# mLSTM cell and gated MLP on one core: seven-product up-projection from the middle of the second chunk, GpSimd's sums re-laid

## The chip, the cores and the metric

The kernel runs on one core of a Trainium2 chip. The metric is the device time of one execution in microseconds (us). The kernel before has a median of 506.22 us in three runs (503.96 to 506.45).

## The reference, cut to what matters

Two blocks follow each other. The first is an mLSTM cell over 768 time steps for 4 x 8 heads of dimension 40; the second is an MLP over the 3072 rows that come out.

```python
for t in range(S):                       # S = 768, per batch and head
    m_new = max(f + m, i)                # running maximum of the gates
    C = exp(f + m - m_new) * C + exp(i - m_new) * outer(v, k)
    n = exp(f + m - m_new) * n + exp(i - m_new) * k
    y[t] = sigmoid(o) * (C @ q) / max(|n . q|, 1)
x = y as (4 * 768, 320)
h = x @ w_in                             # 320 x 2048
out = (h * cos(h)) @ w_out               # 2048 x 320
```

All of it is float32.

## The kernel before, in words

**Chunks and cells.** Time is cut into NC = 6 chunks of 128 steps. A *cell* n = 4c + b is batch b of chunk c, its 8 heads together. A cell is computed in chunkwise form: scores q.k (`scores`, L560, TensorE), times a decay matrix E (`decay_exponents` on GpSimd, L462; `decay` on ScalarE, L476, eight exponentials; `weigh` on VectorE, L566), then `values` (TensorE, L586 to L595: E against v, and the carried state against qG, which `scale_q` makes on GpSimd, L542), `seam` (L701, the increment of the state), `normalize_turned` (VectorE, L613 to L638), `fade` (GpSimd, L684) and `state` (VectorE, L726). `turn_blocks` (VectorE, two transposes, L538) lays out q and k of the next cell.

**Up.** The 512 rows of a chunk (4 batches of 128) go through w_in in 8 *steps* f2 = 0 to 7; a step makes two tiles of 128 features by 512 rows in two PSUM banks. Step "2.6" below is chunk 2 (counted from 0), f2 = 6. In chunks 0 and 1 (class `Up`) a step is four products of 512 columns (two halves of the 256 main input rows, two tiles; L749) and two products over the 64 rows left (`w_in_l`, L743). Each float32 product stands as two matmul records in the trace. In chunks 2 to 5 (class `UpFast`) a step does the 2 x 2 block product with seven products of 256 columns (L817), and the 64-row products (L833). They need sums of blocks of w_in: S1, S2 and S4 in a tile `room`, and S3 written over the block A21 of w_in itself (`up_weight_sums`, L785 to L792, GpSimd), and sums of blocks of x: T1, T2, T4 in `x_room`, and one block of xT overwritten (`x_sums`, L801 to L804, GpSimd). After the first four products ScalarE copies both banks into a tile s (L825, L826), GpSimd makes three sums in s (L834 to L836), and `join` on VectorE (L842, L844) adds them back. TensorE goes on meanwhile with two products of the down-projection (`fill_in`, FILL = 2) and then the last three products of the step; the first of these three writes into the bank that L825 has copied.

**Gate.** h * cos(h) is `near` (ScalarE, L757), `rest` (VectorE, L760), `sin` (ScalarE, L765) and `gate` (L769 on VectorE; in `UpFast` the second tile's gate is on GpSimd, L852).

**Down.** Chunk 0 uses plain products (L863). Chunks 1 to 5 use a block scheme with seven products of 160 columns over sums of g (`sums`, four operations of VectorE, L902 to L905, or of GpSimd) and of w_out (`weight_sums`, GpSimd, L891 to L894, four parts for two pairs each). The products of pair k (L1014) come out of a generator, twelve for a pair, two records each; `down_slot` says how many a step takes. In chunk 1 step f2 takes the 12 products of pair f2 - 1.

**The order of the work** is written out by hand: every engine runs its instructions strictly in the order in which the program lists them. `both_parts` lists the work of one cell and two steps for chunk 1, `both_parts_fast` for chunks 2 to 5. In chunk 1 the cells 8 to 11 are computed, in chunk 2 the cells 12 to 15. The first pair of steps in `both_parts_fast` has a case of its own, `first`, since the scores of its cell are not there yet.

Of the kernel before, what the change touches and what calls it, by code (L numbers as in the profile page):

```python
# [16 lines left out]
OP = mybir.AluOpType  # L17
# [12 lines left out]
def kernel(  # L30
# [355 lines left out]
    def sigmoid_in_place(c):  # L386
        nc.scalar.activation(out=raw_o[c], in_=raw_o[c], func=AF.Sigmoid)
# [384 lines left out]
    wi = w_in_sb.rearrange("p i (f e n) -> p i f e n", e=2, n=128)  # L772
    A11, A12, A21, A22 = (wi[:, i, :, e] for e in range(2) for i in range(NK))
    HB = B // 2 * C
    fast = 2
    Sw, Tx = {}, {}
    x_room = const.tile([128, 3 * B // 2, C], FP, name="x_room")

    def up_weight_sums(part):

        tt = nc.gpsimd.tensor_tensor
        S1, S2, S4 = (room[:, i] for i in range(3))
        Sw[0] = S1, S2, S4, A21
        if part == 0:
            tt(out=S1, in0=A21, in1=A22, op=OP.add)  # L785
            tt(out=S2, in0=S1, in1=A11, op=OP.subtract)
        elif part == 1:
            tt(out=S4, in0=A12, in1=S2, op=OP.subtract)
        r = ((), range(0, 4), range(4, NF // 2))[part]
        if r:  # L790
            r = slice(r[0], r[-1] + 1)
            tt(out=A21[:, r], in0=A11[:, r], in1=A21[:, r], op=OP.subtract)  # L792

    def x_block(c, i, t):
        h = NK * B // 2
        return xT[c][:, i + h * t:h * (t + 1):NK]

    def x_sums(c):
        T1, T2, T4 = Tx[c] = x_room.rearrange("p (k b) t -> k p b t", k=3)
        tt = nc.gpsimd.tensor_tensor  # L800
        tt(out=T1, in0=x_block(c, 0, 1), in1=x_block(c, 0, 0), op=OP.subtract)  # L801
        tt(out=T2, in0=x_block(c, 1, 1), in1=T1, op=OP.subtract)
        tt(out=T4, in0=x_block(c, 1, 0), in1=T2, op=OP.subtract)
        tt(out=x_block(c, 0, 1), in0=x_block(c, 1, 1), in1=x_block(c, 0, 1), op=OP.subtract)  # L804

    class UpFast(Up):

# [72 lines left out]
    def out_to(c, b, o):  # L880
        nc.sync.dma_start(out=out[b * S + c * C:b * S + (c + 1) * C], in_=o)

    def weight_sums(part):

        if part == 0:
            for i in range(3):
                T[i] = pc.tile([128, NF // 2, HALF], FP, name=f"T{i}", tag="bits")
        r = ts(part, NF // 8)
        B11, B12, B21, B22 = (wv[:, r, e, h] for e in range(2) for h in range(2))
        T2, T3, T4 = (t[:, r] for t in T)  # L890
        nc.gpsimd.tensor_tensor(out=T3, in0=B22, in1=B12, op=OP.subtract)  # L891
        nc.gpsimd.tensor_tensor(out=B12, in0=B12, in1=B11, op=OP.subtract)
        nc.gpsimd.tensor_tensor(out=T2, in0=B22, in1=B12, op=OP.subtract)
        nc.gpsimd.tensor_tensor(out=T4, in0=B21, in1=T2, op=OP.subtract)  # L894

    def sums(c, k, engine=nc.vector):

# [113 lines left out]
    def run(made, n):  # L1011
        for _ in range(n):
            a, lhs, rhs, start, stop = next(made)
            nc.tensor.matmul(a, lhs, rhs, start=start, stop=stop)  # L1014
# [39 lines left out]

    def filled(c, f2):

        return c >= fast

    def products_of(c):
        if c not in made_of:  # L1060
# [7 lines left out]
    def down_slot(c, f2):  # L1068

        if c == 0:  # L1070
            if f2 > 0:
                down(0, f2 - 1)
            return
        if f2 == 0:
            if c == 1:
                down(0, LAST)
            else:
                run(made_of[c - 1], 12 - 2 * FILL)
            return
        if f2 == 1 and c > 1:  # L1080
            run(late_products(c - 1), NF)
            return
        each = 14 if c == NC - 1 else 12
        quota = [0] * 8
        for m in range(2, 8):
            quota[m] = each * 7 * (m - 1) // 6 - each * 7 * (m - 2) // 6
        if c == NC - 1:
            quota = [0, 0, 14, 14, 14, 14, 14, 21]
        run(products_of(c), each if c == 1 else quota[f2] - FILL * filled(c, f2))

    pw, pmu = (ps_u.tile([128, HP, C], FP, name=name, tag="up") for name in ("pw", "pmu"))

# [354 lines left out]
    def both_parts(c, b):  # L1447

        n = (c + 1) * B + b
        for i in range(2):  # L1450
            f2 = 2 * b + i
            up = Up(c, f2)
            if i == 0:
                scores(n)
            elif n % 2 == 1 and n + 3 < N:
                load_two(n + 3)
            for e in range(2):
                up.near(e)
            for e in range(2):
                up.rest(e)  # L1460
            if i == 0:
                weigh(n)
                decay_exponents(n + 1)
                for e in range(2):
                    up.sin(e)
                    up.gate(e)
                sums(c, f2)
                if b == B - 1:
                    sigmoid_in_place(c + 2)
                decay(n + 1)  # L1470
            else:
                seam_out(n)
                state(n)
                for e in range(2):
                    up.sin(e)
                    up.gate(e)
                sums(c, f2)
                weigh_k(n + 1)
                odd_values(n + 1)
            down_slot(c, f2)  # L1480
            if i == 0:
                values(n)
                seam(n)
                normalize_turned(n)
                fade(n)
                if b < 3:
                    weight_sums(b + 1)
                load_blocks(n + 2)
                load_E(n + 3)
                if b == B - 2:  # L1490
                    load_o(c + 2)
                sin_next()
            else:
                turn_blocks(n + 1)
                if n + 1 < (fast + 1) * B:
                    scale_q(n + 1)
                if b > 0:
                    up_weight_sums(b - 1)
                if b == B - 1:
                    x_sums(c + 1)  # L1500

    def both_parts_fast(c, b):

        n = (c + 1) * B + b
        cell, follows = n < N, n + 1 < N
        first = (c, b) == (fast, 0)
        ahead = {0: 3, B - 1: 2}.get(b, H - 2)
        pool = nc.gpsimd if cell else nc.vector
        for i in range(2):
            f2 = 2 * b + i  # L1510
            up = UpFast(c, f2, lambda: fill_in(c, f2))
            if f2 == 0:
                if cell:
                    place_gates(c + 1)
                if cell and not first:
                    weigh_k(n)
                sin_next()
            if f2 == 2 * B - 2 and c + 2 < NC:
# [2 lines left out]
            if cell and i == 0:  # L1521
                if first:
                    scores(n)
                    scale_q(n)
                else:
                    values(n)
                    seam(n)
                    if f2 > 0 and follows:
                        turn_blocks(n + 1)
                if follows:  # L1530
                    decay_exponents(n + 1)
            if cell and i == 1:
                if follows:
                    decay(n + 1, range(ahead, H))
                    sin_next()
                    if f2 > 1:
                        scores(n + 1)
                if n % 2 == 1 and n + 3 < N:
                    load_two(n + 3)
                if b == B - 1:  # L1540
                    x_sums(c + 1)
                    if follows:
                        scale_q(n + 1)
                elif follows:
                    weigh_k(n + 1)
                    odd_values(n + 1)
                    scale_q(n + 1)
                if b == 0:
                    if first:
                        fade(n)  # L1550
                    sums(c, 0, pool)
            up.join()
            if first and i == 0:
# [11 lines left out]
            for e in range(2):  # L1565
                up.sin(e)
                up.gate(e)
            if f2 == 0 and follows:
                turn_blocks(n + 1)
            if f2 == 1 and cell:  # L1570
                state(n)
            if f2 == 0 and not cell:
                sums(c, 0, pool)
            if f2 == 2:
                sums(c, 1, pool)
            down_slot(c, f2)
            if f2 == 1 and follows:
                scores(n + 1)
            if f2 == 0:
                for p in range(2):  # L1580
# [3 lines left out]
            if cell and i == 0:  # L1584
                if follows:
                    decay(n + 1, range(ahead))
                if first:
                    values(n)
                    seam(n)
                normalize_turned(n)  # L1590
                if n + 2 < N:
                    load_blocks(n + 2)
                if n + 3 < N:
                    load_E(n + 3)
                if b == B - 2 and c + 2 < NC:
                    load_o(c + 2)
            if i == 0:
                if f2 > 0:
                    if cell:
                        state(n)  # L1600
                    sums(c, f2)
            if i == 1:
# [12 lines left out]
    with tc.manual_schedule():  # L1615
        first_cells()
        first_period()
        for b in range(1, B):
            first_parts(b)
        for c in range(1, NC):  # L1620
            for b in range(B):
                (both_parts_fast if c >= fast else both_parts)(c, b)
        run(made_of[NC - 1], 21)
        combine_last()

# [29 lines left out]
```

## Time and profile before

The profiled execution took 503.72 us, with a span of 501.9 us between its first and its last instruction. The table gives, for each stretch of it, the busy time of each engine in us:

| Stretch | us | TensorE | VectorE | ScalarE | GpSimd |
|---|---|---|---|---|---|
| start, cells of chunk 0 | 31.9 | 30.32 | 26.02 | 24.53 | 16.45 |
| chunk 0 | 83.3 | 82.44 | 76.93 | 74.34 | 49.34 |
| chunk 1 | 76.8 | 76.80 | 64.78 | 47.64 | 48.10 |
| chunk 2 | 78.9 | 78.90 | 70.16 | 54.29 | 54.21 |
| chunk 3 | 78.0 | 77.99 | 69.44 | 55.15 | 56.86 |
| chunk 4 | 75.8 | 75.48 | 61.91 | 46.10 | 45.76 |
| chunk 5 and end | 77.2 | 73.19 | 51.36 | 30.44 | 29.32 |

How to read the profile: a busy TensorE says only that it has matmuls in flight, so the length of a step is read from the start of its first matmul to the start of the next step's. "Idle before" is the time that an engine stood still ahead of an instruction, and what ended it. A line of the timeline gives the start in us from the span's start, the length, the engine, the line of the program, the operation, and output and inputs.

### The profile page before, as it was taken

To read this page: it belongs to the slowest core of one execution; us is meant where nothing else is said; L and a number is where in the kernel's file an instruction comes from. 1 tells how busy PE (TensorE), PEld (TensorE's weight loads), DVE (VectorE), ACT (ScalarE), POOL (GpSimd) and SP (SyncE) were. 2 spreads that over 40 slices of the span, in tenths; PEclk is the share of its full clock that TensorE was granted. 3 is DMA by queue.
4 is the path that set the end of the run, shared out by engine and by line. 5 is a ranking of instruction groups with operands and counts; after the bars stand their busy time and mean duration, and the time that the engine had idled before them with its cause. 6 is when DMAs were issued, how large, how long until landed. Compare 5 with 4: busy or idle time off the path is not lost.

```text
span 501.9 us, 11143 instructions
## 1 busy us (share of the span) xinstructions
PE 495.1 (99%) x4038; PEld 375.4 (75%) x4038; DVE 420.6 (84%) x842; ACT 332.5 (66%) x646; POOL 300.0 (60%) x394
## 2 busy tenths in 40 slices
PE   9999999999999999999999999999999999999997
PEld 6856656565667668887887888788788888787876
DVE  7899998999878878899889889889979866777565
ACT  6799997878564575765877846777847743443541
POOL 8254557666555576787558877657567446434340
PEclk9999999999999999999999999999999999999999
DMA  9989899997366346129446118628113000010001
GB/s 139 182 223 239 213 224 279 233 217 136 114 178 111 101 120 127 50 86 202 132 125 106 48 54 195 168 83 150 43 35 85 1 7 5 2 54 0 2 0 54
DMA packets 100663, 56.74 MB, mean 113 GB/s; under 512 B 63456, under 2 KB 93360, under 8 KB 100608
## 3 DMA queue, kind: packets, MB, share of 16 engines
q1 hardware_dynamic: 97408, 54.43, 46.8%
q10 hardware_dynamic: 2896, 1.23, 1.0%
q8 instruction: 32, 0.52, 0.5%
q0 software_dynamic: 304, 0.36, 0.3%
q14 instruction: 23, 0.19, 0.1%
HBM read 50.66 MB, written 4.10 MB: 109 GB/s over the span
## 4 chain that ended last, share of the span: by engine, by line
PE 85%; ACT 4%; DVE 3%; DMA 2%; SPq 2%; POOL 2%; issue 1%; DVEq 0%; ACTq 0%; POOLq 0%
PE acc L1014 24%; PE pup L817 17%; PE pup L749 9%; PE po L863 6%; PE pup L833 6%; PE late L1014 5%; PE ps L560 4%; PE pup L743 3%; PE vt L595 2%; PE vt L586 2%; PE pu L701 2%; PE ph L576 1%; DMA E<-M_d 1%; DMA vs<-in_v_dram 1%; DVE n L760 1%
## 5 line engine op out<-in xcount | busy, mean ns | idle before, releaser
L757 ACT ACTIVATE n<-pup 128x512 int32<-128x512 f32 x64 | 37.0, 593 | 84.2 <-DVE pup L842 58.4
L765 ACT ACTIVATE n<-n 128x512 f32<-128x512 f32 x96 | 57.7, 626 | 16.5 <-DVE n L760 12.5
L852 POOL TENSOR_TENSOR g<-g,n 128x512 f32<-128x512 f32 x31 | 39.6, 1278 | 47.5 <-ACT n L765 47.4
L749 PE MATMUL pup<-xT,w_in_sb 128*128 128x512 f32 x128 | 58.7, 601 | 0.3 <-ACT xT L712 0.2
L1014 PE MATMUL acc<-w_out_sb,g 128*128 128x160 f32 x320 | 58.7, 303 | 0.0
L760 DVE SCALAR_TENSOR_TENSOR n<-pup,n 128x512 f32<-128x512 f32 x64 | 43.1, 689 | 18.5 <-ACT n L757 15.9
L834 POOL TENSOR_TENSOR blocks<-blocks 128x256 f32<-128x256 f32 x32 | 25.1, 785 | 54.5 <-ACT blocks L826 54.5
L1014 PE MATMUL acc<-T,g 128*128 128x160 f32 x304 | 56.4, 301 | 0.0
L817 PE MATMUL pup<-xT,w_in_sb 128*128 128x256 f32 x192 | 53.5, 385 | 0.2
L476 ACT ACTIVATE E<-E,tab 128x128 f32<-128x128 f32 x160 | 50.1, 389 | 4.3 <-POOL E L462 4.1
L1014 PEld LDWEIGHTS acc<-w_out_sb,g 128*128 128x128 f32 x320 | 49.0, 190 | 4.7 <-issue 2.7
L769 DVE TENSOR_TENSOR g<-pup,n 128x512 f32<-128x512 f32 x64 | 42.7, 687 | 5.7 <-ACT n L765 4.8
L1014 PEld LDWEIGHTS acc<-T,g 128*128 128x128 f32 x304 | 46.5, 190 | 1.1 <-issue 0.4
L749 PEld LDWEIGHTS pup<-xT,w_in_sb 128*128 128x128 f32 x128 | 23.1, 189 | 30.7 <-issue 30.0
L825 ACT COPY blocks<-pup 128x512 f32<-128x512 f32 x32 | 18.6, 582 | 34.2 <-PE pup L817 33.8
L817 PEld LDWEIGHTS pup<-xT,w_in_sb 128*128 128x128 f32 x192 | 33.8, 189 | 9.6 <-ACT blocks L826 4.4
L817 PE MATMUL pup<-x_room,room 128*128 128x256 f32 x128 | 38.5, 382 | 0.0
L542 POOL TENSOR_TENSOR qG<-t,G 128x512 f32<-128x512 f32 x20 | 26.4, 1321 | 16.7 <-DVE t L538 16.7
L1014 PE MATMUL acc<-T,blocks 128*128 128x160 f32 x160 | 36.2, 308 | 0.2 <-POOL blocks L904 0.2
L863 PE MATMUL po<-w_out_sb,g 128*128 128x320 f32 x128 | 36.2, 436 | 0.1
L833 PE MATMUL pup<-xL,w_in_l 64*128 64x512 f32 x128 | 36.1, 641 | 0.0
L566 DVE TENSOR_TENSOR E<-ps,E 128x512 f32<-128x512 f32 x46 | 29.5, 682 | 5.8 <-PE ps L560 5.6
(227 smaller groups left out, 1210.7 us busy)
## 6 DMA issues: line engine op xcount, KB each, us to landing
E<-M_d SPq DMA_DIRECT2D x20, 512.0 KB, 6.0
qr<-in_q_dram SPq DMA_DIRECT2D x72, 80.0 KB, 2.6
kr<-in_k_dram SPq DMA_DIRECT2D x72, 80.0 KB, 2.2
bits<-in_moe_w_out_dram SPq DMA_DIRECT2D x8, 640.0 KB, 6.2
G<-G_d SPq DMA_DIRECT2D x18, 256.0 KB, 5.7
blocks<-in_moe_w_in_dram SPq DMA_DIRECT2D x32, 128.0 KB, 4.6
out_dram<-o_sb SPq DMA_DIRECT2D x23, 160.0 KB, 1.8
o<-in_o_gate_dram SPq DMA_DIRECT2D x40, 80.0 KB, 4.4
```

The costliest lines, as they stand in the source:

```text
L476: nc.scalar.activation(out=Es[n][:, h], in_=Es[n][:, h], func=AF.Exp, scale=-1.0, bias=tab[:, c, 0, g:g + 1])
L566: nc.vector.tensor_tensor(out=w, in0=pss[n][j], in1=w, op=OP.mult)
L749: nc.tensor.matmul(pu.rearrange("p (b t) -> p b t", b=B), w_in_sb[:, i, ts(2 * f2 + e, 128)], xT[c][:, i:NK * B:NK], start=(i == 0 and not ...
L757: nc.scalar.activation(out=self.n[e], in_=self.pu[e], func=AF.Copy, bias=0.25)
L760: nc.vector.scalar_tensor_tensor(out=self.n[e].bitcast(FP), in0=self.pu[e], scalar=0.25, in1=self.n[e], op0=OP.add, op1=OP.subtract)
L765: nc.scalar.activation(out=r, in_=r, func=AF.Sin, scale=TWO_PI_DOWN)
L769: nc.vector.tensor_tensor(out=g, in0=self.pu[e], in1=self.n[e].bitcast(FP), op=OP.mult)
L817: nc.tensor.matmul(bank[:, part].rearrange("p (b t) -> p b t", b=B // 2), w[:, f2], x, start=start, stop=stop, skip_group_check=True)
L833: nc.tensor.matmul(pu, w_in_l[r, f2], xL[c][r].rearrange("p b t -> p (b t)"), start=False, stop=True, skip_group_check=True)
L852: tt(out=self.g, in0=self.g, in1=self.n[e].bitcast(FP), op=OP.mult)
L863: nc.tensor.matmul(po[c][b], gs[c, f][:, ts(b, C)], w_out_sb[:, f], start=(f == 0), stop=(f == NF - 1))
L1014: nc.tensor.matmul(a, lhs, rhs, start=start, stop=stop)
```

## The change

Chunk 1 goes over to seven products with its fifth step: `FAST = 1, B // 2`, so `both_parts_fast` runs from chunk 1, b = 2 (steps 1.4 to 1.7), and the case `first` moves there from chunk 2, b = 0. In `first`, `scale_q` is already done by `both_parts`, `turn_blocks` and `state` of the cell stand in steps 1.4 and 1.5, `fade` after `values`, and the next cell's scores after the slot of step 1.5, the odd one. The sums for w_in are made in halves over the feature pairs (4 and 4) and moved forward: S1 and S2 in step 1.0, S4, T1, T2, T4 and the upper half of S3 in step 1.2, the x block in step 1.3. The lower half of S3 overwrites what the plain steps 1.0 to 1.3 read, and is made in step 1.7, behind the gates. `weight_sums` of parts 1 and 2 move to steps 1.1 and 1.3, ahead of `scale_q`; part 3 is split over steps 1.5 and 1.6. Step 1.3 takes ten products in its slot in place of twelve, steps 1.4 to 1.7 take two as fill and ten in the slot, and step 2.0 takes two and ten in place of two and eight.

```diff
-    fast = 2
+    FAST = 1, B // 2
...
         Sw[0] = S1, S2, S4, A21
+        halves = slice(0, 4), slice(4, NF // 2)
         if part == 0:
-            tt(out=S1, in0=A21, in1=A22, op=OP.add)
-            tt(out=S2, in0=S1, in1=A11, op=OP.subtract)
+            for r in halves:
+                tt(out=S1[:, r], in0=A21[:, r], in1=A22[:, r], op=OP.add)
+            for r in halves:
+                tt(out=S2[:, r], in0=S1[:, r], in1=A11[:, r], op=OP.subtract)
         elif part == 1:
-            tt(out=S4, in0=A12, in1=S2, op=OP.subtract)
-        r = ((), range(0, 4), range(4, NF // 2))[part]
-        if r:
-            r = slice(r[0], r[-1] + 1)
+            for r in halves:
+                tt(out=S4[:, r], in0=A12[:, r], in1=S2[:, r], op=OP.subtract)
+        else:
+            r = halves[3 - part]
             tt(out=A21[:, r], in0=A11[:, r], in1=A21[:, r], op=OP.subtract)
...
     def filled(c, f2):
-        return c >= fast
+        return (c, f2 // 2) >= FAST
...
-                run(made_of[c - 1], 12 - 2 * FILL)
+                run(made_of[c - 1], 12 - FILL if c == 2 else 12 - 2 * FILL)
...
-        run(products_of(c), each if c == 1 else quota[f2] - FILL * filled(c, f2))
+        run(products_of(c), (each - FILL * (f2 > 2)) if c == 1 else quota[f2] - FILL)
...
# both_parts (chunk 1, now b = 0 and 1 only)
             if i == 0:
                 weigh(n)
                 decay_exponents(n + 1)
+                if b == 1:
+                    up_weight_sums(1)
+                    x_sums(c, [0])
...
                 sums(c, f2)
-                if b == B - 1:
-                    sigmoid_in_place(c + 2)
                 decay(n + 1)
...
                 fade(n)
-                if b < 3:
-                    weight_sums(b + 1)
+                up_weight_sums(2 * b)
                 load_blocks(n + 2)
                 load_E(n + 3)
-                if b == B - 2:
-                    load_o(c + 2)
                 sin_next()
             else:
                 turn_blocks(n + 1)
-                if n + 1 < (fast + 1) * B:
-                    scale_q(n + 1)
-                if b > 0:
-                    up_weight_sums(b - 1)
-                if b == B - 1:
-                    x_sums(c + 1)
+                if b == 1:
+                    x_sums(c, [1])
+                weight_sums(b + 1)
+                scale_q(n + 1)
...
# both_parts_fast
-        first = (c, b) == (fast, 0)
+        first = (c, b) == FAST
...
-                if cell and not first:
+                if cell:
                     weigh_k(n)
...
                 if first:
                     scores(n)
-                    scale_q(n)
...
-                    if f2 > 1:
+                    if f2 > 1 and not first:
                         scores(n + 1)
...
-                    if first:
-                        fade(n)
                     sums(c, 0, pool)
...
             for e in range(2):
                 up.sin(e)
                 up.gate(e)
-            if f2 == 0 and follows:
+            if c == 1:
+                if f2 in (5, 6):
+                    weight_sums(3, range(2 * f2 - 10, 2 * f2 - 8))
+                elif f2 == 7:
+                    up_weight_sums(3)
+            if (f2 == 0 or first and i == 0) and follows:
                 turn_blocks(n + 1)
-            if f2 == 1 and cell:
+            if (f2 == 1 or first and i == 1) and cell:
                 state(n)
...
-            if f2 == 2:
+            if f2 == 2 and c > 1:
                 sums(c, 1, pool)
             down_slot(c, f2)
-            if f2 == 1 and follows:
+            if (f2 == 1 or first and i == 1) and follows:
                 scores(n + 1)
...
                 if first:
                     values(n)
                     seam(n)
+                    fade(n)
...
-                    if cell:
+                    if cell and not first:
                         state(n)
                     sums(c, f2)
```

`x_sums(c, parts)` makes T1, T2 and T4 for part 0 and overwrites the x block for part 1; `weight_sums(part, steps)` runs only the named ones of its four operations.

## The prediction

> **What bounds the kernel now.** I read the page first, then the windows by stage, then the timeline of TensorE around chunks 1 to 3, and last the queues of the other engines. Times are us; "step 1.4" is chunk 1, f2 = 4.
>
> ```profile
> span 501.9 us, 11143 instructions
> PE 495.1 (99%) x4038; PEld 375.4 (75%) x4038; DVE 420.6 (84%) x842; ACT 332.5 (66%) x646; POOL 300.0 (60%) x394
> ...
> PEclk9999999999999999999999999999999999999999
> ```
>
> TensorE works for 99% of the span at the full granted clock. In chunks 1 and 2 it never stands still, so a step costs what its matmuls cost, and whatever makes TensorE wait is added to the time. The other engines have room on average, but chunk 2's VectorE (70.16 of 78.9) has little; it is their order that can bind.
>
> **The gain: TensorE's own floor.** The starts of the steps are 135.25, 146.32, 154.18 in chunk 1: an even plain step takes 11.07, an odd one 7.86. In chunk 2 steps 2.4 and 2.5 (232.42, 242.66, 251.65) take 10.24 and 9.00 with 28 records of the down-projection, 0.136 each by their starts. With chunk 1's 24 that is 9.70 and 8.46. Step 2.0 took 10.12 with 20 records, so the new joint, step 1.4, takes 10.66. Steps 2.0 and 2.1 become what 3.0 and 3.1 are (9.55 + 10.60) and four records: 20.69. Step 1.3 loses four: 7.32.
>
> Before, 1.3 to 2.1: 7.86 + 11.07 + 7.86 + 11.07 + 7.86 + 21.03 = 66.75. After: 7.32 + 10.66 + 8.46 + 9.70 + 8.46 + 20.69 = 65.29. The floor falls by **1.46**, 0.3% of the span. That is all the change can win; every wait that it makes on TensorE counts against it. I now go through the queues for such waits.
>
> **Part 1: the lower half of S3, wait at step 2.0.** It overwrites what steps 1.0 to 1.3 read, and is issued in step 1.7 on GpSimd behind the second gate. Step 2.0 needs it in its second product. The trace has the same hand-over one chunk later, step 2.7 to 3.0:
>
> ```profile
> 268.81 0.73 POOL L803 TENSOR_TENSOR x_room<-xT,x_room 128x256 f32<-128x256 f32 x1
> 269.50 0.73 POOL L804 TENSOR_TENSOR xT<-xT 128x256 f32<-128x256 f32 x1
> 270.19 1.73 POOL L542 TENSOR_TENSOR qG<-t,G 128x512 f32<-128x512 f32 x1
> 271.87 1.28 POOL L852 TENSOR_TENSOR g<-g,n 128x512 f32<-128x512 f32 x1
> ...
> 270.89 0.59 PE L817 MATMUL pup<-x_room,room 128*128 128x256 f32 x2
> 271.32 1.30 PE L817 MATMUL pup<-xT,w_in_sb 128*128 128x256 f32 x4
> ...
> 179.83 1.28 POOL L792 TENSOR_TENSOR w_in_sb<-w_in_sb 128x512 f32<-128x512 f32 x1
> ```
>
> The gate (L852) ends at 273.15, 1.8 after TensorE began its second product at 271.32. A half of S3 (L792, 1.28) behind it would end at 274.4: a wait of 3.1. In chunk 1 the step is 0.54 shorter by its four records: 3.6. GpSimd can't be earlier by itself: from step 1.7's start it has the copies at 2.6, then three sums (2.4), four x sums (3.2), scale_q (1.3), gate and S3 (1.28 each): 12.1, against 8.9 for TensorE. Where VectorE is late as well (below) it grows to 4.5. Bounds 3.2 to 5.0; I take **4.2**. TensorE runs in order, so nothing hides it; later steps have no idle time to give it back.
>
> **Part 2: the ten products in step 1.3.** TensorE would reach step 1.4 at 153.64 in place of 154.18. But its first product needs a bank that the first gate of step 1.3 still reads: L769 starts at 153.25, takes two tiles in 1.29, and frees the first at 153.94. So 0.4 to 0.54 of the saving is a wait; **0.5**.
>
> **Part 3: GpSimd beside `sums`.** Where all four `sums` of VectorE (both inputs in SBUF) run while GpSimd adds, they double:
>
> ```profile
> 154.58 0.43 DVE L902 TENSOR_TENSOR blocks<-g 128x256 f32<-128x256 f32 x1
> ...
> 264.78 0.77 DVE L902 TENSOR_TENSOR blocks<-g 128x256 f32<-128x256 f32 x1
> 265.58 0.83 DVE L903 TENSOR_TENSOR g<-g 128x256 f32<-128x256 f32 x1
> 266.34 0.94 DVE L904 TENSOR_TENSOR blocks<-blocks,g 128x256 f32<-128x256 f32 x1
> 267.31 0.83 DVE L905 TENSOR_TENSOR blocks<-g,blocks 128x256 f32<-128x256 f32 x1
> ```
>
> 3.4 for four in place of 1.7; GpSimd's 0.73 became 0.79 to 0.90. In chunk 1 GpSimd used to be idle at that moment. Now, from the end of fade (128.19), come S1 and S2 in four halves (1.28 each, 5.1), weigh_k (0.72), and four `weight_sums` (0.94 apart): busy to 137.7. The `sums` of step 1.1 start at 135.64, so about 1.0 is lost, and the transposes behind them end 1.0 later:
>
> ```profile
> 138.20 1.08 DVE L538 STREAM_TRANSPOSE t<-kr 128x512 f32<-128x512 f32 x1
> ...
> 139.74 1.06 PE L560 MATMUL ps<-t,t 40*128 40x128 f32 x16
> ```
>
> They end at 139.28, the scores start at 139.74; at 140.3 they hold TensorE in step 1.2 for about 0.7. Bounds 0 (no doubling) and 1.1; **0.7**. In step 1.2 the S4 halves and x sums (6.5 together, before fade) do the same, but VectorE's 1.68 of idle time ahead of step 1.3's rest takes it. Halving by itself costs about 0.1 an operation and is hidden.
>
> On this contention the Trainium skill, "SBUF — State Buffer", section "Who interferes with whom", says that a VectorE instruction with two SBUF inputs contends with a reading GpSimd instruction, and that the loser blocks fully. The trace agrees that they contend, but 0.84 against 0.42 is less than a full block by a 0.73 operation would make; by the rule the term would be about 1.1.
>
> **Part 4: the joint, steps 1.4 to 1.7.** The model is step 2.0, with offsets from its start, 192.04. There GpSimd's sums ran at once (+2.6), join ended at +5.9, the second sine at +9.0, then ScalarE loaded the exponential and made three, and the next step's copies began at 203.62. Now `scale_q` stands ahead of the sums and waits for a VectorE transpose:
>
> ```profile
> 157.35 1.27 POOL L542 TENSOR_TENSOR qG<-t,G 128x512 f32<-128x512 f32 x1 [5.55 <-DVE t L538]
> ...
> 202.73 0.99 ACT L476 ACTIVATE E<-E,tab 128x128 f32<-128x128 f32 x3
> 203.62 0.56 ACT L825 COPY blocks<-pup 128x512 f32<-128x512 f32 x1
> ```
>
> So the sums run from 158.6 (+4.4), join ends at +7.5 and the second sine at +10.6. `ahead` is six for b = 2: table 1.28, six exponentials 1.86, so step 1.5's first copy ends at +14.3. TensorE needs it at 10.66 + 2.27 = +12.9. With the second copy: 1.55; bounds 0.8 to 2; **1.5**.
>
> VectorE is behind as well. After step 1.4's gate (+10.8) stand transposes (2.0), normalize (3.1, as in 203.79 to 206.92) and `sums` (1.7 alone, 3.3 beside GpSimd's sums, weigh_k and scale_q), so step 1.5's join starts at +17.5 to +19.1, and its gate ends 3.7 later (247.60 to 251.26 in step 2.5). TensorE's third product of step 1.6 wants that gate's bank at +21.5: 0 to 1.3 of wait; nearer the upper end, since GpSimd has work throughout, **1.1**.
>
> Step 1.6 has its transposes behind `sums` and weigh; its second sine ends about when step 1.7 starts, where in step 2.6 it was 1.1 earlier. Table and two exponentials then put step 1.7's copies about 1 late: 0 to 1.5; **0.8**. The weight_sums in steps 1.5 and 1.6 (1.9 each) are ready before their slots and cost only through GpSimd's queue, counted above. SP's loads keep their places and come earlier than needed; sigmoid of the output gates in step 1.6 runs while ScalarE waits for join.
>
> **Sum.** 4.2 + 0.5 + 0.7 + 1.5 + 1.1 + 0.8 = 8.8 of waits, less 1.46: **+7.3**. The profiled execution took 503.72 (span 501.9, 1.8 around it); the median shown is 506.22, 2.5 above. The same step gives 511.0 on the first and 513.5 on the second; I predict the middle, 512.3.
>
> **Rivals.**
> *A, the forecast:* several waits, +4.5 to +10. For it: orders that no slack covers. Chance 0.60.
> *B, only the certain waits:* VectorE and ScalarE keep up (no doubling, join at its old offset), and what is left is S3 at 3.2 to 3.7 and 0.5: +2.3 to +2.8, 506 to 509. For it: VectorE is busy only 15.3 of 18.93 in a pair of chunk 1. Against it: scale_q's wait is in the order itself. Chance 0.18, two thirds of it above the bound.
> *C, full blocking:* a two-input operation of VectorE waits out GpSimd's (0.73 to 1.28) each time, so four take about 4.7 in place of 3.4; by 1.2 more at three places (steps 1.2, 1.5, 1.7): about +11, 515 to 517. This is the skill's rule just cited. One L903 at 163.73 took 1.19 beside a 1.30 mask, which speaks for it; the four above speak against. Chance 0.10.
> *D, not slower:* the floor shows. Place: GpSimd's queue in step 1.7. It decides from the point where the lower S3 ends within 8.9 of that step's start, that is if GpSimd's operations there take 3.2 less than their rows say (spans on POOL are rough). Then -1.46, with the small waits about 502 to 506. Chance 0.12, a quarter of it faster by the bound.
> That step 1.4 is not switched over is excluded by the comparison that selects it.
>
> **How the numbers follow.** A measurement of this kernel can tell about 0.5% (2.5 us) from no change. Slower: 0.60 + 0.12 + 0.10 = 0.82; same: 0.06 + 0.09 = 0.15; faster: 0.03. The range leaves out most of D and the edge of C: 507 to 517.
>
> **What would show it.** A GpSimd release ahead of step 2.0's second product of 3 to 5; a ScalarE copy releasing step 1.5's fifth product; scores in step 1.2 released by a VectorE transpose; TensorE idle near 9 between 135 and 225, where it was none. Wrong if step 2.0 follows 1.7 without a gap, or if chunk 1 ends near 191.

## The result, and the profile after

The changed kernel takes a median of 519.18 us in four runs (517.90 to 521.85); the kernel before took 505.14 in four (503.96 to 506.45). The ratio is 1.0284, with a 95% interval of 1.0231 to 1.0337: **14.0 us slower**, where 512.3 and a range of 507 to 517 were forecast.

Above the first changes the line numbers are those of the kernel before; further down they are a few higher, and one more in some experiments: in the changed kernel L822 are the seven products, L795 is S3, L830 and L831 are ScalarE's copies, L839 to L841 GpSimd's three sums, L847 and L849 `join`, L906 to L909 `sums`, L1018 the products of the down-projection.

The page of the profiled execution (521.85 us) has these lines:

```profile
span 520.0 us, 11244 instructions
PE 502.8 (97%) x4062; PEld 385.2 (74%) x4062; DVE 428.7 (82%) x846; ACT 339.2 (65%) x656; POOL 319.5 (61%) x417
...
PEclk9899999999999979899999999999999999999999
```

TensorE is no longer in flight for 99% of the span, and the granted clock, which stood at 9 in every slice before, falls to 7 in the slice from 182 us and to 8 in that from 208 us (and in that from 13 us, below). This execution is the longest of the four: 3.3 of its 18.1 us of extra span lie ahead of chunk 1, where the two kernels do the same work, and where a stretch of half clock at 17.67 us stands. That isn't put down to the change: of the experiments on the changed kernel the second (at 18.33) and the third (at 18.15) have such a stretch, and the others have none. Steps 1.0 to 2.1 alone take 111.48 in place of 97.90: **+13.6**, which is the difference of the medians to 0.5. A last 1.2 lies behind step 2.1, in small pieces down to the end.

TensorE's waits in chunk 1 and the first two steps of chunk 2 (who waited on which line, the sum, how often, the longest):

```profile
PE pup L822 <- POOL w_in_sb L795: 3.5, 1, 3.5
PE ps L560 <- DVE st L726: 2.4, 1, 2.4
PE pup L822 <- ACT blocks L830: 1.1, 1, 1.1
PE ps L560 <- DVE t L538: 0.6, 1, 0.6
PE pup L822 <- DVE g L769: 0.3, 1, 0.3
```

Together 7.9 (8.0 with a gap of 0.12 in step 1.5). The windows of steps 1.5, 1.6, 1.7 and 2.0 (each line has the window, its length, the busy time and the number of instructions of TensorE, its weight loads, VectorE, ScalarE and GpSimd, then the granted clock, and the share and GB/s of the DMA):

```profile
169.06:183.44 14.38, 10.76 (x63) 8.19 (x59) 11.67 (x25) 8.47 (x17) 10.20 (x13) 0.93 0.52 133
183.44:195.62 12.18, 12.18 (x116) 10.01 (x115) 8.41 (x18) 8.58 (x11) 6.05 (x10) 0.80 0.17 52
195.62:204.07 8.45, 8.45 (x60) 7.11 (x59) 8.14 (x16) 6.50 (x15) 7.46 (x11) 1.00 1.09 185
204.07:219.16 15.09, 11.62 (x116) 9.25 (x115) 9.65 (x15) 7.33 (x15) 11.31 (x14) 0.89 0.17 53
```

The steps that nothing disturbs are close to the forecast: 8.45 for 8.46 here, 10.74 for 10.66 in step 1.4, 10.84 for 10.60 in step 2.1. Step 1.6 is the odd one. TensorE is busy in all of its 12.18, waits for nothing, and has 9.70 of work: its clock is 0.80. Cut at the points where the clock changes, the trace shows only 1.00 and 0.50:

```profile
178.10:181.51 3.41, 0.97 (x8) 0.63 (x7) 2.72 (x7) 1.70 (x3) 1.10 (x2) 1.00 0.19 50
181.51:184.92 3.41, 3.41 (x18) 2.92 (x19) 1.71 (x4) 0.00 (x0) 1.89 (x3) 0.50 0.24 65
184.92:188.34 3.42, 3.42 (x11) 2.97 (x10) 3.03 (x5) 1.60 (x3) 0.37 (x1) 0.50 0.00 0
188.34:191.75 3.41, 3.41 (x50) 2.22 (x53) 0.89 (x2) 3.38 (x3) 3.19 (x5) 1.00 0.00 0
205.41:208.82 3.41, 0.69 (x3) 0.64 (x4) 3.28 (x6) 0.00 (x0) 3.12 (x4) 1.00 0.01 2
208.82:212.23 3.41, 3.41 (x12) 2.89 (x11) 0.76 (x2) 2.30 (x5) 0.97 (x2) 0.50 0.00 0
```

Read TensorE's busy time, right behind the length, against the clock, third from the end: where TensorE was busy for only 0.97 or 0.69 of 3.41 us, the stretch behind runs at half clock. The 3.42 us at half clock from 184.92 hold 11 matmul records, the next 3.41 at full clock 50 (shorter ones among them). The changes of the clock lie on one grid: 17.67, 181.51 and 208.82 are 48 and 8 periods of 3.413 us apart. In steps 1.5 to 2.0 the half clock lasts 10.24, with TensorE busy throughout, and half of it, **5.1**, is lost time. So of the 13.6: 8.0 waits, 5.1 clock, less the 1.46 of the floor, and 1.9 that is left (1.3 of it in step 1.5, where TensorE starts again three times; 0.4 of that is there without any wait as well, as the last two runs show; the rest is not resolved).

### The profile page after: what moved, and what is told of

Its sections match the earlier page's. It is cut to its first block, busy times and chain, and to the rows that moved or that the text cites. A ratio compares the mean times of both kernels' runs of the same rounds, so it can differ in the third digit from the quotient of the medians.

```text
span 520.0 us, 11244 instructions
## 1 busy us (share of the span) xinstructions
PE 502.8 (97%) x4062; PEld 385.2 (74%) x4062; DVE 428.7 (82%) x846; ACT 339.2 (65%) x656; POOL 319.5 (61%) x417
## 4 chain that ended last, share of the span: by engine, by line
PE 77%; DMA 6%; DVE 6%; ACT 4%; POOL 3%; SPq 2%; issue 1%; ACTq 0%; DVEq 0%; POOLq 0%
PE acc L1018 22%; PE pup L822 20%; PE pup L838 7%; PE pup L749 5%; PE late L1018 4%; PE ps L560 4%; PE po L868 3%; PE vt L595 2%; PE vt L586 2%; DMA bits<-in_moe_w_out_dram 2%; PE pup L743 1%; PE ph L576 1%; PE pu L701 1%; DMA ks<-in_k_dram 1%; ACT n L757 1%
## 5 line engine op out<-in xcount | busy, mean ns | idle before, releaser
L857 POOL TENSOR_TENSOR g<-g,n 128x512 f32<-128x512 f32 x35 | 44.7, 1277 | 53.3 <-ACT n L765 53.2
L839 POOL TENSOR_TENSOR blocks<-blocks 128x256 f32<-128x256 f32 x36 | 28.2, 785 | 61.6 <-ACT blocks L831 61.6
L822 PE MATMUL pup<-xT,w_in_sb 128*128 128x256 f32 x216 | 61.6, 393 | 3.7 <-POOL w_in_sb L795 3.5
L1018 PE MATMUL acc<-w_out_sb,g 128*128 128x160 f32 x320 | 59.1, 304 | 0.0
L1018 PE MATMUL acc<-T,g 128*128 128x160 f32 x304 | 57.9, 303 | 0.0
L1018 PEld LDWEIGHTS acc<-w_out_sb,g 128*128 128x128 f32 x320 | 48.8, 190 | 4.6 <-issue 2.5
L760 DVE SCALAR_TENSOR_TENSOR n<-pup,n 128x512 f32<-128x512 f32 x60 | 40.5, 689 | 12.3 <-ACT n L757 9.8
L822 PEld LDWEIGHTS pup<-xT,w_in_sb 128*128 128x128 f32 x216 | 38.9, 193 | 15.2 <-ACT blocks L831 5.4
L1018 PEld LDWEIGHTS acc<-T,g 128*128 128x128 f32 x304 | 47.6, 192 | 1.7 <-issue 0.4
L830 ACT COPY blocks<-pup 128x512 f32<-128x512 f32 x36 | 20.9, 582 | 41.8 <-PE pup L822 41.6
L822 PE MATMUL pup<-x_room,room 128*128 128x256 f32 x144 | 44.9, 394 | 0.3 <-DVE g L769 0.3
L749 PE MATMUL pup<-xT,w_in_sb 128*128 128x512 f32 x96 | 44.0, 601 | 0.5 <-DVE g L769 0.3
L847 DVE TENSOR_TENSOR pup<-pup,blocks 128x256 f32<-128x256 f32 x36 | 15.7, 436 | 32.4 <-PE pup L838 30.2
L838 PE MATMUL pup<-xL,w_in_l 64*128 64x512 f32 x144 | 40.6, 641 | 0.0
L1018 PE MATMUL acc<-T,blocks 128*128 128x160 f32 x160 | 36.2, 308 | 0.3
L560 PEld LDWEIGHTS ps<-t,t 40*128 40x128 f32 (+1 forms) x384 | 26.1, 192 | 12.6 <-issue 9.7
```

The costliest lines, as they stand in the source:

```text
L560: nc.tensor.matmul(ps[j][:, p], kT[r, p], qT[r, p], start=True, stop=True)
L749: nc.tensor.matmul(pu.rearrange("p (b t) -> p b t", b=B), w_in_sb[:, i, ts(2 * f2 + e, 128)], xT[c][:, i:NK * B:NK], start=(i == 0 and not ...
L760: nc.vector.scalar_tensor_tensor(out=self.n[e].bitcast(FP), in0=self.pu[e], scalar=0.25, in1=self.n[e], op0=OP.add, op1=OP.subtract)
L822: nc.tensor.matmul(bank[:, part].rearrange("p (b t) -> p b t", b=B // 2), w[:, f2], x, start=start, stop=stop, skip_group_check=True)
L838: nc.tensor.matmul(pu, w_in_l[r, f2], xL[c][r].rearrange("p b t -> p (b t)"), start=False, stop=True, skip_group_check=True)
L857: tt(out=self.g, in0=self.g, in1=self.n[e].bitcast(FP), op=OP.mult)
```

## The experiments

Theory at the start: the largest wait is the order of the lower half of S3; the waits of steps 1.4 to 1.7 come from the joint's new place, whose work stands in VectorE's and GpSimd's queues there; and a long wait is paid a second time by the clock behind it. The rivals: TensorE would be held at 2.0 by something else as well; the seven products make these waits wherever the joint lies; a wait costs just its length. All runs but the last two are single ones beside one run of the kernel before on the same chip (504.39 for the first four, 503.56 for the next four).

**Lower half of S3 early.** To the changed kernel:

```diff
                 weight_sums(b + 1)
+                if b == 1:
+                    up_weight_sums(3)
                 scale_q(n + 1)
...
-                elif f2 == 7:
-                    up_weight_sums(3)
```

> The changed kernel with one operation moved: the lower half of S3 is made in step 1.3, right after the weight sums and ahead of scale_q, where GpSimd waits for a transpose anyway, in place of behind the last gate of step 1.7. Theory (waits count twice): the wait of 3.47 us ahead of step 2.0's second product goes, and with it the 3.41 us stretch at half clock that follows it, so step 2.0 falls from 15.09 to 10.1 and the span by about 5.0. Rival (the half clock comes from the seven-product steps in chunk 1, not from waiting): step 2.0 falls by 3.5 only and a half-clock stretch stays between 200 and 220 us. Steps 1.5 and 1.6 stay at 14.4 and 12.2 by both.

513.36 us. Step 2.0 fell from 15.09 to 10.53. Its second product, the one that needs S3, starts at 200.80 without a wait. The timeline of TensorE at its third:

```profile
201.95 0.70 PE L822 MATMUL pup<-xT,w_in_sb 128*128 128x256 f32 x2 [0.56 <-DVE g L769]
```

Only a 0.56 wait for a gate of VectorE is left, and no half clock behind it. One order on GpSimd cost 4.6 us: 3.5 as wait, 1.7 as clock, less the 0.56 that it had covered. Steps 1.5 and 1.6, expected to stay at 14.4 and 12.2, took 13.71 and 11.46: behind their wait the half clock lasted one period of 3.41 in place of two.

**The state one step earlier.** In step 1.5 the scores wait for `state`, which frees the PSUM bank they write, and `state` stands behind the gate. Here `state` goes ahead of step 1.4's `sums`, as in the other pairs:

```diff
-            if (f2 == 1 or first and i == 1) and cell:
+            if f2 == 1 and cell:
                 state(n)
...
-                    if cell and not first:
+                    if cell:
                         state(n)
```

> The changed kernel with the joint's state addition (cell 10) put back into the even step 1.4, behind normalize and ahead of the sums; the scores stay at the end of step 1.5. Theory: the scores of step 1.5 waited 2.44 us for a PSUM bank that held the state's increment, and the clock halved for 6.83 us because of that wait. Both go: steps 1.5 and 1.6 together fall from 26.56 to 19.4 to 20.5 (the copy's wait of 1.06 stays, and VectorE's gate may bring up to 1.1 in step 1.6). Rival (the scores wait for VectorE's late weigh or join, whatever holds the bank): VectorE has 0.9 more ahead of its join, step 1.5 stays within 1 us of 14.4.

520.17 us. Steps 1.5 and 1.6 took 24.04, more than the theory allowed; step 1.5 stayed at 14.24, as the rival had it. The scores wait no longer; the wait moved to the products of the down-projection ahead of them:

```profile
PE acc L1018 <- DVE blocks L908: 2.1, 1, 2.1
```

`sums` now ends later by `state` and by a longer L908 (1.48 in place of 0.94). So the bank was the place where it showed, and VectorE's queue behind step 1.4 the likely cause, which the run that relieves this queue bears out below. The half clock came as well, at 178.76.

**More work in place of the wait.** The first product of step 2.0 is done nine times over instead of once (the same numbers are written each time):

```diff
-            product(b1, second, S2, T2, True, True)
+            for _ in range(9 if (c, f2) == (2, 0) else 1):
+                product(b1, second, S2, T2, True, True)
```

> The changed kernel with added work: the first product of step 2.0 is done nine times in place of once (the same numbers are written again), 16 more records of 0.216 us, 3.45 us, which lie where TensorE waits for S3. Theory (the clock halves because TensorE stood still): no half-clock stretch follows, and step 2.0 takes 13.4 to 13.7 in place of 15.09, so added work makes it shorter by about 1.5. Rival (the clock's fall has another cause, or waiting costs its own length only): step 2.0 takes 15.1 or more.

517.95 us. Sixteen more matmul records made step 2.0 shorter, 13.66 in place of 15.09, as the theory had it. The last line is the start of step 2.1:

```profile
201.82 4.05 PE L822 MATMUL pup<-x_room,room 128*128 128x256 f32 x18
206.11 1.13 PE L822 MATMUL pup<-xT,w_in_sb 128*128 128x256 f32 x4 [0.24 <-POOL w_in_sb L795]
...
215.48 0.59 PE L822 MATMUL pup<-x_room,room 128*128 128x256 f32 x2
```

The half clock behind 2.0 is gone, the one at 181.99 is still there. A wait that costs its length could not give this: the same time would have been spent either way.

**A wait where there was none.** To the kernel before, at the end of step 2.7, half of S2 is made anew (the same numbers once more):

```diff
+            if (c, f2) == (2, 7):
+                S1, S2 = Sw[0][0:2]
+                nc.gpsimd.tensor_tensor(out=S2[:, 0:4], in0=S1[:, 0:4], in1=A11[:, 0:4], op=OP.subtract)
```

> The kernel before with one added GpSimd operation: the lower half of S2 is made once more (the same numbers) behind the last gate of step 2.7. Step 3.0's first product then waits for it, with nothing else changed. By the rows the gate ends at 273.15 and the added 1.28 at 274.4, against 270.89: a wait of 3.5 to 3.6. Theory: step 3.0 grows by 4.5 to 5.5, since a half-clock stretch of 3.41 us follows. Rival (waiting costs its own length): by 3.5 to 3.7, granted clock 1.0 throughout.

508.85 us, and here the rival was right, with a little less than its 3.5. Steps 2.7 and 3.0 took 21.78 in place of 18.55: +3.2 for a wait of 3.36 (L1570 is the added operation), and no half clock behind it.

```profile
276.11 0.70 PE L817 MATMUL pup<-x_room,room 128*128 128x256 f32 x2 [3.36 <-POOL room L1570]
```

The one change of clock in this run is at its end, at 506.63, where TensorE is done. On a grid of 3.413 counted back from there a period ends at 274.53, so that 1.8 of the wait lay in one and 1.6 in the next.

**The same, all of S2.** To the kernel before, with `out=S2, in0=S1, in1=A11` whole:

> The kernel before with the whole of S2 (2.36 us) made once more behind the last gate of step 2.7, in place of its half. With the half, step 3.0 waited 3.36 and the clock stayed at 1.0, since the wait lay across two of the 3.41 us periods at whose ends the clock changed in the earlier runs (1.8 and 1.6 in each). Now the wait is 4.5, so that at least one period has 2.2 or more of it. Theory (the clock halves for the next period when TensorE stood still for about 2 or more of one): steps 2.7 and 3.0 together grow from 21.8 to 24.4 to 25, of which 1.1 is the longer wait and 1.5 to 1.7 the clock. Rival (waits cost their length): to 22.9, clock 1.0.

511.59 us. Steps 2.7 and 3.0 took 25.52 in place of 18.55: **7.0 for a wait of 4.42**. The windows by periods:

```profile
271.64:275.05 3.41, 0.30 (x3) 0.06 (x1) 2.91 (x5) 0.88 (x2) 3.41 (x3) 1.00 0.28 79
275.05:278.46 3.41, 2.09 (x5) 1.74 (x6) 2.73 (x4) 0.00 (x0) 1.71 (x2) 0.50 0.00 0
278.46:281.88 3.42, 3.42 (x11) 2.88 (x11) 0.00 (x0) 2.23 (x5) 0.90 (x2) 0.50 0.00 0
```

A period with 0.30 of work, then 6.83 at half clock, with the full clock back behind it. The theory, with one period at half clock, had 24.4 to 25. So in a kernel without the change, too, a wait's price has a second term. Whether it falls due does not go by the length alone: 3.36 split over two periods brought no half clock, 2.44 inside one did in the changed kernel.

**The joint back at 2.0.** Seven products from 1.4, S3 early, and the order of chunk 1 otherwise plain; the long edit's core, to the first experiment:

```diff
+    JOINT = 2
...
-            up = Up(c, f2)
+            up = UpFast(c, f2, lambda: fill_in(c, f2)) if seven else Up(c, f2)
...
+            if seven:
+                up.join()
+                if i == 0:
+                    weigh(n)
...
-        first = (c, b) == FAST
+        first = (c, b) == (JOINT, 0)
```

> Seven products from step 1.4 on, as in the changed kernel, with the lower half of S3 made in step 1.3, but the joint left where it was, at step 2.0: the cells of chunk 1 keep their plain order (scores in the even step, state and transposes in the odd one). Kernel to compare: the run e1, with the joint at 1.4, where steps 1.4 to 1.7 took 11.35 + 13.71 + 11.46 + 8.45 = 44.97. The floor of the four steps by the rows is 36.3. Theory (what is left after S3 is VectorE's double load at the joint: one cell's transposes and weigh more, and sums that the very next step's products need): the four steps take 36.3 to 39, no wait over 1.5, no half clock. Rival (seven products in chunk 1 overload GpSimd or VectorE wherever the joint is): 42 or more.

515.83 us. Steps 1.4 to 1.7 took 45.28, in the first experiment 44.97. So my theory that the joint's new place makes the waits falls: without it the four steps take as long, with other waits (5.3 in place of 4.0), one of 2.13 among them with 3.41 at half clock behind it. In chunk 1 and the first steps of chunk 2 the largest sum is:

```profile
PE ps L560 <- DVE t L538: 3.8, 3, 2.1
```

The scores wait for VectorE's transposes (3.8); products wait for ScalarE's copies (1.9) and VectorE's gates (1.6) where the plain order is kept. That speaks for the rival: the seven products themselves, with their copies, sums and join between product and gate, leave the three slower engines little room here. It is argued, not shown, for the order counts as well: the run with three cures below takes most of the waits away with the joint at 1.4.

**`scale_q` behind the three sums of the copies.** To the first experiment; in step 1.4 GpSimd makes L839 to L841 first:

```diff
-                scale_q(n + 1)
+                if b == 0:
+                    scale_q(n + 1)
...
                     scores(n)
+                    scale_q(n)
```

> The run e1 with scale_q of cell 10 put back behind the three sums of step 1.4 on GpSimd, as the joint had it before. Theory (VectorE's queue sets the scores of step 1.5: join, weigh, rest, gate, transposes, normalize, sums, join, rest, gate, state without a pause): join of step 1.4 comes 1.1 to 1.5 earlier, the copy's wait of 1.27 in step 1.5 goes, and the scores still wait 2 to 3 for the state; steps 1.4 and 1.5 fall from 25.06 to 23.5 to 24. Rival (the waits are independent, and the late scale_q is behind all of them): the scores' wait falls below 1.2 as well, and the two steps to 22.5 or less.

512.68 us. Steps 1.4 and 1.5 took 23.76 (25.06 in the first experiment), as expected, and the wait for the copies is gone; the scores still wait 2.43 for `state`. But step 1.6 took 12.44 in place of 11.46: the wait lay wholly inside a period, and 6.83 at half clock followed, where the first experiment had 3.41. What the edit won, the clock took back.

**`scale_q` ahead of the weight sums in step 1.1.** To the first experiment, so that GpSimd is idle while `sums` runs:

```diff
+                if b == 0:
+                    scale_q(n + 1)
                 weight_sums(b + 1)
```

> The run e1 with scale_q ahead of the weight sums in step 1.1, so that GpSimd stands still while VectorE makes the sums of step 1.1. Theory (GpSimd's reads slow VectorE's operations with two SBUF inputs): the four sums fall back to about 1.7 us in all, the transposes end before the scores, the wait of 0.64 in step 1.2 goes, and step 1.2 takes 11.1 in place of 12.06; GpSimd is 3.8 later from there on, with 0 to 1 of it given back in step 1.4. Rival (the transposes are late for another reason): step 1.2 stays at 12.

516.28 us. Step 1.2 is back at 11.07, and its wait is gone. The two middle ones of VectorE's four sums, first in the timeline of the changed kernel, beside GpSimd's weight sums:

```profile
139.46 0.96 DVE L907 TENSOR_TENSOR g<-g 128x256 f32<-128x256 f32 x1
140.35 1.08 DVE L908 TENSOR_TENSOR blocks<-blocks,g 128x256 f32<-128x256 f32 x1
```

and in this run, with GpSimd idle:

```profile
137.32 0.42 DVE L907 TENSOR_TENSOR g<-g 128x256 f32<-128x256 f32 x1
137.66 0.42 DVE L908 TENSOR_TENSOR blocks<-blocks,g 128x256 f32<-128x256 f32 x1
```

The 1.2 us between them are GpSimd's doing. They were given back with more: GpSimd starts its next list later, and steps 1.3 and 1.4 grow to 8.63 and 12.76 (waits of 1.15 and 1.55) from 7.77 and 11.35.

**Three cures together.** To `scale_q` behind: `state` in step 1.4 as above, and its `sums` on GpSimd. Four executions, and six of the kernel before:

```diff
-                    sums(c, f2)
+                    sums(c, f2, nc.gpsimd if first else nc.vector)
```

> The run e6 with VectorE relieved at the joint: the sums of step 1.4 go to GpSimd (3.2 there in place of 1.7 to 3.1 on VectorE), and the state addition of cell 10 stands in step 1.4, ahead of them. Theory (VectorE's unbroken queue from the join of 1.4 to the state held the scores of step 1.5, and the half clock followed from that wait): the scores no longer wait, steps 1.4 to 1.6 fall from 36.2 to 29 to 31.5, no half-clock stretch near 180; about 5 us less than e6, 1 to 3 us above the kernel before. Rival (GpSimd can't carry it: its sums for step 1.5 come later by as much, and the wait goes to join or to the slot): steps 1.4 to 1.6 stay above 34.

Median 508.47 (508.01 to 509.90), the kernel before 503.99: ratio 1.0083 [1.0065, 1.0101]. Steps 1.4 to 1.6 took 29.82, as expected (37.30 in the changed kernel), and the clock is whole there. The whole came out worse than expected: 4.5 above the kernel before, where 1 to 3 was forecast. The windows of steps 1.5 and 1.7 (columns as above):

```profile
167.16:176.01 8.85, 8.85 (x63) 7.05 (x59) 6.60 (x17) 6.26 (x14) 7.75 (x12) 1.00 0.66 168
185.83:195.73 9.90, 9.02 (x61) 7.05 (x59) 9.44 (x22) 8.40 (x17) 8.31 (x10) 1.00 0.98 171
```

Step 1.5 has no wait left. It is at step 1.7 now (9.90 against 8.46), where VectorE is busy for 9.44 of 9.90.

**Twelve products in step 1.3**, two and eight in 2.0, to the last. Again four executions:

```diff
-                run(made_of[c - 1], 12 - FILL if c == 2 else 12 - 2 * FILL)
+                run(made_of[c - 1], 12 - 2 * FILL)
...
-        run(products_of(c), (each - FILL * (f2 > 2)) if c == 1 else quota[f2] - FILL)
+        run(products_of(c), (each - FILL * (f2 > 3)) if c == 1 else quota[f2] - FILL)
```

> The run e10 with twelve products left in the slot of step 1.3 and two and eight in step 2.0, as before the change. Theory (the ten products only bring TensorE earlier to a bank that the gate of step 1.3 still reads): step 1.3 grows by 0.1 at most to 7.86, step 2.0 falls by 0.5, the whole is 0.3 to 0.5 less than e10. Rival (the fill of steps 1.4 to 1.7 then waits for GpSimd's gate, whose result its second product reads): a wait ahead of the fill in step 1.5 or 2.0 takes the 0.5 back or more.

Median 508.63, ratio 1.0088 [1.0062, 1.0115]. The wait at the hand-over (0.29) is gone and steps 1.0 to 2.1 take 101.32 in place of 101.69, as expected; in the whole time that can't be seen. The longest that is left in TensorE's waits:

```profile
PE pup L822 <- DVE g L769: 0.6, 1, 0.6
PE ps L560 <- DVE t L538: 0.6, 1, 0.6
```

No version that was run beats the kernel before. The last one is 3.4 above it in these steps and 4.9 above its own floor. Besides the two shown there are 0.5 for a copy of ScalarE and 0.4 for another gate of VectorE, and the four sums in step 1.6 still take 1.07, 0.97, 0.95 and 0.84, twice as long as alone. All waits above 0.1 add up to 2.4 of the 4.9. Part of the rest is the floor itself, which was set too low (next section). That GpSimd's w_in and w_out sums beside VectorE make the waits that are left is argued from these rows; it wasn't tried to take all of them away.

## Why the prediction was wrong, point by point

The direction and the places of four of the six waits were right; the time was not. That the waits' sum came close (8.0 for 8.8) is luck: two of the waits didn't come, and one of 2.44 came that is in no term.

- **The floor.** Right to 0.1 in steps 1.4 and 1.7. Step 1.5 took 8.85 without a wait in the last two runs, 0.39 more than its 8.46, and step 2.1 10.84, 0.24 more than its 10.60: by these two the gain to be had was nearer 0.8 than 1.46. It showed nowhere as a gain.
- **Part 1, S3.** 4.2 forecast (3.2 to 5.0), 3.47 measured as a wait. The replay of GpSimd's queue from the hand-over of chunk 2 to 3 held; the first experiment took the wait away, with only 0.56 for a gate behind it. The step failed in what it left out: the sum counts a wait at its length, and this one cost 1.7 more.
- **Part 2, the hand-over.** 0.5 forecast, 0.29 measured.
- **Part 3, sums beside GpSimd.** 0.7 forecast, a wait of 0.62, the step longer by 0.89. The two middle sums took 0.96 and 1.08, more than the 0.84 taken from the trace before. Rival C's full block is in the trace too: single sums took 1.48 (L908 with the state one step earlier) and 1.57 (L906 in the run with `scale_q` ahead) beside GpSimd's operations of 0.9 to 1.4. So the Trainium skill's rule in "SBUF — State Buffer", section "Who interferes with whom", that the loser of the shared port blocks fully, fits these two operations, while a back-to-back row such as 0.83, 0.94, 0.83 comes out below it. C itself fell: its time, 515 to 517, was close, but not its mechanism, as the clock and the wait for `state` made the difference.
- **Part 4, the copies in step 1.5.** 1.5 forecast, 1.06 measured. The replay was close: copy ended at +14.3 by the working, and in the timeline at 172.60, +14.3.
- **Part 4, VectorE behind.** The times were right and the consequence wrong. Forecast: join of step 1.5 at +17.5 to +19.1, its gate's end 3.7 later. The trace:

```profile
176.92 0.42 DVE L847 TENSOR_TENSOR pup<-pup,blocks 128x256 f32<-128x256 f32 x1
...
180.50 0.85 DVE L726 TENSOR_TENSOR st<-st,pu 40x128 f32<-40x128 f32 x4
...
181.49 2.02 PE L560 MATMUL ps<-t,t 40*128 40x128 f32 x14 [2.44 <-DVE st L726]
```

Join at 176.92 is +18.6, the gate (0.69 from 179.89) ends at 180.58, +22.2. But behind the gate stands `state`, which ends at 181.35, and the scores, moved by the change into this step's end, need its bank: TensorE stood ready at 179.05 and started at 181.49. The prediction asked only for the gate's own bank at step 1.6. The wait for that (1.1) and the copies in 1.7 (0.8) didn't come, probably since the 2.44 and the half clock ahead of them moved TensorE back and let the others catch up. The run with three cures agrees for the second: the scores no longer wait there, and step 1.7 has a wait of 0.76 for a copy:

```profile
189.41 0.70 PE L822 MATMUL pup<-x_room,w_in_sb 128*128 128x256 f32 x2 [0.76 <-ACT blocks L830]
```

- **The clock.** This is the step that failed. The prediction said "whatever makes TensorE wait is added to the time" and had no term for the clock; it read PEclk as constant because it stood at 9 everywhere, in a profile where TensorE didn't wait in chunks 1 and 2. The half clock behind the waits made 5.1 of the 13.6, and most of the miss of 6.9 (519.18 against 512.3). The Trainium skill, "TensorE: Matmul & The Clock Gate", section "What's actually happening", describes free-running windows of 3413 ns and two states of the clock; the grid and the two values here agree. The Trainium skill, on the same page in the section "HAM oscillation — how this bites in real kernels", gives as the rule that TensorE should have no gap above about 3.4 us. By that rule only the 3.47 at step 2.0 could have counted; here a wait of 2.44 was followed by 6.83 at half clock, and one of 3.36 by none.

The forecast with the clock in it (7.3 + 5.1 = 12.4) would have given about 517. That sum is made afterwards, and it too has a sum of waits that is right by luck.

## What to carry to other kernels

Where TensorE is the bound and never waits, its clock in the profile is that of a kernel that never waits: price a new wait of about 2 us or more at its length and, if it may fall inside one 3.4 us period, at 1.7 to 3.4 more (half of the 3.41 or 6.83 at half clock seen here). When a consumer is moved (here the scores), look up every tile it writes, and follow that tile's last reader in its own engine's queue, behind all that the change has made late. Before a scheme that saves TensorE time is extended by four steps, add up what it asks of the other engines there: 1.46 of TensorE's time was bought with copies, sums and joins for which VectorE and GpSimd, slowing each other, had too little room in the orders tried.

## What the hardware showed that was not expected

- The clock halved behind waits of 2.1 to 2.4 us (steps 1.5 or 1.6 of seven runs), and not behind 3.36 that was split 1.8 and 1.6 over two periods. In the first experiment only 1.84 of a 2.43 wait lay in the deciding period, with 1.06 of scores (40 of 128 rows) behind it, and the clock halved all the same. That scores count for less than full products would fit, and also that the half clock lasted two periods where the scores fell into the first of them (the changed kernel, `scale_q` behind) and one where most were done before (the third and the `scale_q` ahead run); the run with the joint back, with 0.47 us of scores done before, lies between and has one. It wasn't tried apart. Nor is standing time alone the rule at the start of the program: in the third experiment TensorE stood still for only 1.12 of the 3.41 us ahead of the half clock at 18.15, with products of 41 columns (L576) beside it, less than the 1.78 that brought no half clock in the run with half of S2.
- Work can be cheaper than waiting: 16 more matmul records shortened step 2.0 by 1.4.
- One VectorE sum of 128 x 256 with both inputs in SBUF took from 0.42 us with GpSimd idle to 1.57 beside GpSimd's operations.
